# A transformer block's front, fed pair by pair: scale, shift and q weights in k-tile pairs, and no bias pass

## Chip, cores, metric

One core of a Trainium2 chip. The time is device microseconds (us) of one execution. Before the change: 841.25 us, median of three runs (841.21 to 841.26).

PE is the matmul engine, DVE the vector engine, ACT the scalar engine, POOL the GpSimd engine, SP the queue that issues DMA transfers. "Half clock" below means that the profile reads a granted PE clock of 0.50, or, where it reads 1.00 all the same, that matmuls start at half their pace. In the kernel before those of 512 columns start 0.426 us apart at a reading of 0.50 and 0.218 at 1.00. A *k-tile* is 128 of the 1024 rows over which a matmul sums, an *x tile* 128 rows of x. A *PSUM bank* is a buffer into which these kernels' matmuls add up; ACT and DVE read it out (an *evacuation*) before the program uses it again (in b1 PE waited 1.53 us for that). The *z matmuls* sum phi(k) over the rows; they are the first work after chunk 0's k and the first part of chunk 1's.

## The reference, cut to what matters

```python
x = A_x                                           # (1, 2048, 1024), bf16
mod = (silu(c) @ w_mod).reshape(1, 6, 1, -1)      # w_mod: (1024, 6144)
sa, ca, ga, sb, cb, gb = (mod[:, i] for i in range(6))
h = layernorm(x) * (1 + ca) + sa                  # ca: scale, sa: shift
qkv = h @ wqkv                                    # 32 heads of 32
# phi(q), phi(k), linear attention, @ wo, residual;
# then a second modulated layernorm and a SwiGLU block of width 3584
```

Only the first four lines' way into q matters here. The sequence is worked on in four chunks of 512 rows; the *front* is everything up to the end of chunk 0's q and k.

## The kernel before

Every instruction is recorded through a small helper that works out the waits, so all of them carry one line number (L178); the profile has to be read by tile names. The parts that the change touches:

```python
# loads, all on one queue, in this order
for st in range(4):
    P.dma("x0_%d" % st, XRES[:, st, :], xv[:, st, :])
P.dma("wca0", WCA[:, :, 0:512], wmv[:, :, D:D + 512])         # scale, rows of 1 KB
P.dma("wq0", WQK[:, 0:4, 0:512], wqkvv[:, 0:4, 0:512])
P.dma("wq1", WQK[:, 0:4, 512:D], wqkvv[:, 0:4, 512:D])
P.dma("wca1", WCA[:, :, 512:D], wmv[:, :, D + 512:2 * D])
P.dma("wq2", WQK[:, 4:8, 0:D], wqkvv[:, 4:8, 0:D])
P.dma("wsa", WSA[:], wmv[:, :, 0:D])                          # shift, rows of 2 KB
# ... x tiles 4, 5, first half of wk, x tiles 6, 7, second half of wk

def mod_sc(w, c0, ms):                 # silu(c) @ w_mod: matmuls of one column
    for m in ms:
        for kt in range(NDT):
            P.pe("matmul", out=PS[:, 0, c0 + m:c0 + m + 1], lhsT=w[:, kt, m * 128:(m + 1) * 128],
                 rhs=SILUC[:, kt:kt + 1], ...)

def q_bias(nts):                       # shift @ Wq, again one column each
    for nt in nts:
        for dt in range(NDT):
            P.pe("matmul", out=PS[:, 0, 16 + nt:17 + nt], lhsT=WQK[:, dt, nt * 128:(nt + 1) * 128],
                 rhs=MODTMP[:, dt:dt + 1], ...)
    P.dve("tensor_copy", out=BQ[...], in_=PS[...])

def q_phase_chunk0(side):              # q from h without the shift; the shift comes in as a bias
    lo, hi = [2, 0, 3, 1], [6, 4, 7, 5]
    for nt in range(7):
        q_part(nt, 1 + nt, lo)         # 4 matmuls 128x128x512 into PSUM bank 1 + nt
        if nt == 4:
            mod_sc(WCA, 8, range(4, NDT)); fin_ca(1)
            for dt in hi: h0_scale(dt, HT[:, 1, dt, :])
    for nt in range(6):
        q_part(nt, 1 + nt, hi)
    mod_sc(WSA, 0, range(NDT))
    act_stats(4); ...                  # LayerNorm statistics of x tiles 4, 5 (chunk 1)
    fin_sa()
    q_part(6, 7, hi)
    q_bias([0, 1])
    ...
    q_bias([2, 3, 4, 5, 6, 7])
    ...
    for dt in range(NDT):              # eight adds: k needs h with the shift
        P.dve("tensor_scalar", out=HT[:, 1, dt, :], in0=HT[:, 0, dt, :], scalar1=MODCOL[:, 1, dt:dt + 1], ...)
    for nt in range(2):
        phi_evac(1 + nt, PQT[:, nt, 0:512], bias=BQ[:, nt:nt + 1])   # ACT exp and relu, DVE min and add
    q_part(7, 1, range(NDT))           # needs bank 1 back
    for nt in range(2, 8): ...
```

Chunk 1 is prepared meanwhile: statistics, normalisation on DVE, a transposing DMA into tile `ht`, then eight scale/shift operations on `ht`, half on DVE and half on ACT.

## Time and profile before

| | before |
|---|---|
| time | 841.25 us |
| span of the profiled run | 839.5 us |
| first q matmul | 13.34 us |
| first k matmul of chunk 0 | 33.71 us |
| the first z matmul, after 80 k matmuls (64 of chunk 0, 16 of chunk 1) | 51.33 us |

The page of the kernel before: span, busy time of the engines, and the chain of work that ended last.

```profile
span 839.5 us, 10310 instructions
...
PE 827.5 (99%) x4211; PEld 384.3 (46%) x4291; DVE 295.9 (35%) x627; ACT 210.2 (25%) x363; POOL 41.3 (5%) x51
...
PE 94%; SPq 2%; DMA 1%; DVE 1%; issue 1%; ACT 0%; DVEq 0%; ACTq 0%
```

PE is busy 99% of the span and is 94% of the chain: the kernel is bound by matmuls nearly everywhere. A gain can only come from stretches where PE waits, does work that it need not do, or runs at half clock.

The stretches of the front. The columns are the stretch, its length, then busy us (and instructions) of PE, PE's weight loads, DVE, ACT and POOL, then the granted PE clock, the busy share of the DMA engines, and GB/s.

```profile
8.00:13.00 5.00, 3.79 (x67) 2.97 (x68) 3.47 (x15) 1.45 (x3) 2.04 (x3) 1.00 1.08 359
13.00:25.00 12.00, 11.92 (x84) 5.71 (x84) 2.37 (x9) 3.28 (x6) 0.00 (x0) 1.00 1.06 378
25.00:34.00 9.00, 8.13 (x143) 5.15 (x144) 5.88 (x24) 7.29 (x13) 0.74 (x1) 0.81 0.83 275
...
31.00:32.00 1.00, 1.00 (x3) 0.30 (x2) 1.00 (x5) 1.00 (x3) 0.42 (x1) 0.50 0.76 248
...
242.00:243.00 1.00, 1.00 (x6) 0.45 (x5) 0.62 (x3) 0.00 (x0) 1.00 (x3) 1.00 1.16 291
```

Two things to see. From 8 us on the DMA engines are full (a busy share of 1.06 to 1.08), at 359 to 378 GB/s. And around 31 us the granted clock is 0.50. The last line is from much later, where the only traffic is the gate and up weights, whose pieces have rows of 512 bytes: the engines are just as full (1.16) and move 291 GB/s. Single microseconds of this trace in which only 2 KB rows move (19 to 24 us) show 383 to 389, those with 1 KB rows (11 to 13 us) 348 and 349, about 350.

The timeline of PE for the front: start and length in us, then engine, operation, and tiles, and in brackets the idle time before, with what ended it. `siluc,wca` and `siluc,wsa` are the one-column matmuls for scale and shift, `modtmp,wqk` is the bias pass, `ht,wqk` is q, `wqk,ht` is k. The next start time minus this one, divided by the count, is the real pace; a group's length includes the tail of its last matmul (one of 512 columns is recorded as 0.379 us long on average).

```profile
13.34 4.52 PE L178 MATMUL ps<-ht,wqk 128*128 128x512 bf16 x20
...
25.41 1.74 PE L178 MATMUL ps<-siluc,wsa 128*128 128x1 bf16 x64
27.23 0.81 PE L178 MATMUL ps<-ht,wqk 128*128 128x512 bf16 x3
28.16 0.55 PE L178 MATMUL ps<-modtmp,wqk 128*128 128x1 bf16 x16
28.97 1.35 PE L178 MATMUL ps<-modtmp,wqk 128*128 128x1 bf16 x48 [0.26 <-DVE mv L178]
30.73 3.15 PE L178 MATMUL ps<-ht,wqk 128*128 128x512 bf16 x7 [0.41 <-ACT rl L178]
...
33.71 17.78 PE L178 MATMUL ps<-wqk,ht 128*128 128x512 bf16 x79
51.33 0.24 PE L178 MATMUL ps<-ones,pk_87 128*128 128x1 bf16 x4
```

Twenty q matmuls start over 4.36 us (13.34 to 17.70), 0.218 each; the k matmuls further on 0.216. The seven recorded in the line at 30.73 (eight are issued; some matmul records are missing from a trace) start over 2.98 us, 0.426 each: half clock. Before them lie 128 one-column matmuls and only four real ones.

The chain of waits of the kernel before also shows two pieces that are not PE:

```profile
46.15 0.80 ACT ht L178
...
47.81 1.52 ACT ht L178 x2
```

ACT is still scaling chunk 1's tile `ht` when PE gets there. The 80 k matmuls from 33.71 to 51.33 us take 17.62 us, 0.35 more than at 0.216 each.

### The profile page before, as it was taken

The numbers are of one execution on the slowest core, as the hardware profiler recorded it, in microseconds if no ns is written. First come the engines' busy times: TensorE is split into PE (matmuls) and PEld (weight loads), VectorE is DVE, ScalarE is ACT, GpSimd is POOL, SyncE is SP. The second block draws the span as 40 slices with busy tenths as digits, with TensorE's granted clock in tenths as the row PEclk, the third lists the DMA queues.
The fourth block names the chain that finished last, engine by engine and source line by source line (L and its number), as shares of the span: only waits on it lengthen the run. The fifth ranks groups of instructions, "written<-read, shape, count | busy, mean of one in ns | idle before, by whom it ended". The sixth has DMA issues, their size and how long they took to land.

```text
span 839.5 us, 10310 instructions
## 1 busy us (share of the span) xinstructions
PE 827.5 (99%) x4211; PEld 384.3 (46%) x4291; DVE 295.9 (35%) x627; ACT 210.2 (25%) x363; POOL 41.3 (5%) x51
## 2 busy tenths in 40 slices
PE   8999999999999999999999999999999999999998
PEld 4544444444444444444444444444444444444444
DVE  4677866656984211111221111022111202111111
ACT  5677763313333111100111111021111101111111
POOL 1000000000050000030000003000000300000000
PEclk9999999999999999999999999999999999999999
DMA  9792323746195895530355552045556204553000
GB/s 311 221 322 51 60 105 126 166 142 251 50 246 175 262 300 155 156 87 25 102 156 152 154 154 61 26 114 150 151 151 157 69 13 113 151 152 98 1 26 26
DMA packets 173391, 113.02 MB, mean 135 GB/s; under 512 B 32536, under 2 KB 156576, under 8 KB 173344
## 3 DMA queue, kind: packets, MB, share of 16 engines
q1 hardware_dynamic: 173344, 112.35, 47.4%
q8 instruction: 34, 0.56, 0.3%
q14 instruction: 13, 0.11, 0.0%
HBM read 100.67 MB, written 4.33 MB: 125 GB/s over the span
## 4 chain that ended last, share of the span: by engine, by line
PE 94%; SPq 2%; DMA 1%; DVE 1%; issue 1%; ACT 0%; DVEq 0%; ACTq 0%
PE ps L178 94%; SPq L178 2%; DMA xres<-in_A_x_dram 1%; DVE acc L178 0%; ACT ht L178 0%; DVE xres L178 0%; DVE mhl L178 0%; DVE stats L178 0%; ACT mw L178 0%; ACT e_92 L178 0%; DVE ve_72 L178 0%; ACT rl L178 0%; DVE ut L178 0%; DVE mv L178 0%; DVE mean_70 L178 0%
## 5 line engine op out<-in xcount | busy, mean ns | idle before, releaser
L178 DVE TENSOR_TENSOR at<-sg,ps 128x512 bf16<-128x512 bf16 x112 | 77.0, 687 | 296.2 <-PE ps L178 285.1
L178 ACT ACTIVATE sg<-ps 128x512 bf16<-128x512 f32 x112 | 66.9, 597 | 310.3 <-PE ps L178 298.9
L178 PE MATMUL ps<-wd_a,at 128*128 128x512 bf16 (+2 forms) x519 | 112.8, 372 | 0.5
L178 PE MATMUL ps<-wd_b,at 128*128 128x512 bf16 (+2 forms) x388 | 85.4, 372 | 0.5
L178 PEld LDWEIGHTS ps<-wd_a,at 128*128 128x128 bf16 x528 | 51.1, 98 | 59.8
L178 DVE TENSOR_TENSOR ut<-att,gb_b 128x512 bf16<-128x512 bf16 (+1 forms) x32 | 13.9, 434 | 167.3 <-ACT att L178 167.3
L178 ACT ACTIVATE att<-ps 128x512 bf16<-128x512 f32 (+1 forms) x32 | 17.4, 592 | 182.1 <-PE ps L178 182.1
L178 PEld LDWEIGHTS ps<-wd_b,at 128*128 128x128 bf16 x396 | 38.3, 98 | 44.6
L178 PE MATMUL ps<-ht,wqk 128*128 128x512 bf16 x248 | 57.8, 386 | 0.8 <-ACT rl L178 0.4
L178 PE MATMUL ps<-wqk,ht 128*128 128x512 bf16 x250 | 57.0, 379 | 0.5
L178 PE MATMUL ps<-mw,pqt 128*128 128x512 bf16 x250 | 55.8, 379 | 0.4
L178 PE MATMUL ps<-h2t,guu_117 128*128 128x512 bf16 x221 | 52.8, 379 | 0.2
L178 PE MATMUL ps<-h2t,guu_115 128*128 128x512 bf16 x219 | 52.6, 379 | 0.3
L178 PE MATMUL ps<-h2t,gug_114 128*128 128x512 bf16 x220 | 52.6, 379 | 0.2
L178 PE MATMUL ps<-h2t,guu_116 128*128 128x512 bf16 x221 | 52.6, 379 | 0.2
L178 PE MATMUL ps<-h2t,gug_111 128*128 128x512 bf16 x220 | 52.5, 379 | 0.2
L178 PE MATMUL ps<-h2t,gug_112 128*128 128x512 bf16 x219 | 52.5, 379 | 0.2
L178 PE MATMUL ps<-h2t,gug_113 128*128 128x512 bf16 x219 | 52.3, 379 | 0.3
L178 PE MATMUL ps<-h2t,guu_118 128*128 128x512 bf16 x217 | 52.1, 379 | 0.3
L178 POOL TENSOR_SCALAR h2t<-h2t,modcol 128x512 bf16<-128x512 bf16 x32 | 28.6, 911 | 395.8 <-DMA h2t<-xn_119 395.8
L178 ACT ACTIVATE e_92<-ps 128x512 bf16<-128x512 f32 x56 | 33.6, 600 | 27.0 <-PE ps L178 24.5
L178 PEld LDWEIGHTS ps<-mw,pqt 128*128 128x128 bf16 x256 | 24.9, 98 | 29.7 <-DVE xres L178 0.2
(123 smaller groups left out, 707.7 us busy)
## 6 DMA issues: line engine op xcount, KB each, us to landing
gug_111<-in_B_w_gate_dram SPq DMA_DIRECT2D x14, 512.0 KB, 4.0
guu_115<-in_B_w_up_dram SPq DMA_DIRECT2D x14, 512.0 KB, 5.3
gug_112<-in_B_w_gate_dram SPq DMA_DIRECT2D x14, 512.0 KB, 4.1
guu_116<-in_B_w_up_dram SPq DMA_DIRECT2D x14, 512.0 KB, 5.3
gug_113<-in_B_w_gate_dram SPq DMA_DIRECT2D x14, 512.0 KB, 4.0
guu_117<-in_B_w_up_dram SPq DMA_DIRECT2D x14, 512.0 KB, 5.3
gug_114<-in_B_w_gate_dram SPq DMA_DIRECT2D x14, 512.0 KB, 4.0
guu_118<-in_B_w_up_dram SPq DMA_DIRECT2D x14, 512.0 KB, 5.2
```

What stands on the lines that cost most here:

```text
L178: return getattr(e, method)(**kw)
```

## The change

The front is to be limited by PE alone: shift is added where scale is applied, so the bias pass goes (64 one-column matmuls and their waits), and so do the eight adds. For this, scale and shift must come early: they arrive in pairs of k-tiles with the q weights of that pair. q begins with two row tiles, at half width, as soon as pair 0 is there. Chunk 1's x is loaded before the k weights, and its scale/shift operations all go to DVE. The diff holds more than that: the last eight q matmuls use PSUM bank 0 instead of waiting for bank 1, the scaling of chunk 0 goes wholly to DVE, and statistics and later loads change places.

The core of the diff (cuts marked, lines shortened):

```diff
-        P.dma("wca0", WCA[:, :, 0:512], wmv[:, :, D:D + 512])
-        P.dma("wq0", ...)  P.dma("wq1", ...)  P.dma("wca1", ...)  P.dma("wq2", ...)
-        P.dma("wsa", WSA[:], wmv[:, :, 0:D])
+        def ca_load(p):
+            P.dma("wca%d" % p, WCA[:, :, 256 * p:256 * p + 256], wmv[:, :, D + 256 * p:D + 256 * p + 256])
+        def wq_load(p):
+            P.dma("wq%d" % p, WQK[:, 2 * p:2 * p + 2, 0:D], wqkvv[:, 2 * p:2 * p + 2, 0:D])
+        def sa_load(p):
+            P.dma("wsa%d" % p, WSA[:, :, 256 * p:256 * p + 256], wmv[:, :, 256 * p:256 * p + 256])
+        for p in range(4):
+            ca_load(p)
+            sa_load(p)
+            if p < 3:
+                wq_load(p)
+        # ... the last two q k-tiles one by one, x tiles 4 to 7, then wk
 ...
-        def q_bias(nts): ...
+        def mod_pair(p):
+            mod_sc(WCA, 8, range(2 * p, 2 * p + 2)); mod_sc(WSA, 0, range(2 * p, 2 * p + 2))
+            for f in fin_ca(p): f()                       # five small DVE operations
+            for dt in range(2 * p, 2 * p + 2): h0_scale(dt)   # scale and shift in one
 ...
         def q_phase_chunk0(side):
+            for nt in range(5):
+                q_part(nt, qb[nt], (0, 1), 0, 256)        # row tiles 0, 1 only
+            tile_transposes(2); tile_transposes(3)
+            ...
+            for nt in range(5):
+                if nt == 3: mod_pair(1)
+                q_part(nt, qb[nt], (0, 1), 256, 512)
+            for nt in range(5, 7): q_part(nt, qb[nt], (0, 1))
             for nt in range(7):
+                if nt == 4: mod_pair(2)
+                q_part(nt, qb[nt], (2, 3))
+            for nt in range(7):
+                if nt == 4: mod_pair(3)
+                q_part(nt, qb[nt], (4, 5))
+            act_stats(4); ...
+            for nt in range(6): q_part(nt, qb[nt], (6,))
+            for nt in range(7):
+                q_part(nt, qb[nt], (7,) if nt < 6 else (6, 7))
+                phi_evac(qb[nt], PQT[:, nt, 0:512])       # no bias
 ...
-            if dt % 2 == 0:
+            if dt % 2 == 0 or ch == 1:                    # chunk 1: all on DVE
 ...
-        warm(14)
+        warm(11, bank=3)                                  # warm-up matmuls, then wait for pair 0
```

More of the change, by code (lines that the diff above doesn't have):

```diff
@@ L396, in bass_adaLN_cond__linear_attn_block__swiglu_ffn__prompt_kernel @@
             P.dma("x0_%d" % st, XRES[:, st, :], xv[:, st, :])
-        P.dma("wca0", WCA[:, :, 0:512], wmv[:, :, D:D + 512])
-        P.dma("wq0", WQK[:, 0:4, 0:512], wqkvv[:, 0:4, 0:512])
-        P.dma("wq1", WQK[:, 0:4, 512:D], wqkvv[:, 0:4, 512:D])
-        P.dma("wca1", WCA[:, :, 512:D], wmv[:, :, D + 512:2 * D])
-        P.dma("wq2", WQK[:, 4:8, 0:D], wqkvv[:, 4:8, 0:D])
-        P.dma("wsa", WSA[:], wmv[:, :, 0:D])
-        for j in range(2):
+        def ca_load(p):
[9 more added lines that the diff above has]
+                wq_load(p)
+        for i in range(6, 8):
+            P.dma("wq%d" % i, WQK[:, i, 0:D], wqkvv[:, i, 0:D])
+        for j in range(4):
             P.dma("x1_%d" % j, XRES[:, 4 + j, :], xv[:, 4 + j, :])
-        P.dma("wk0", WQK[:, :, 1024:1536], wqkvv[:, :, 1024:1536])
-        for j in range(2, 4):
-            P.dma("x1_%d" % j, XRES[:, 4 + j, :], xv[:, 4 + j, :])
+        for i in range(2):
+            P.dma("wk0%d" % i, WQK[:, 4 * i:4 * i + 4, 1024:1536], wqkvv[:, 4 * i:4 * i + 4, 1024:1536])
         P.dma("wk1", WQK[:, :, 1536:2048], wqkvv[:, :, 1536:2048])
@@ L437, in bass_adaLN_cond__linear_attn_block__swiglu_ffn__prompt_kernel @@
         P.act("activation", out=SILUC[:], in_=PSB[:, 1, 0:NDT], func=ACT.Silu)
-        P.act("activation", out=ACTWARM[:], in_=SILUC[:], func=ACT.Exp)
         P.dve("tensor_copy", out=SILUF[:], in_=SILUC[:])
@@ L468, in th_dma @@
         def th_dma(st):
-            buf, j = (st // 4 + 1) % 2, st % 4
+            buf, j = (st // 4) % 2, st % 4
             xbar(HT[:, buf, :, j * 128:(j + 1) * 128], XRES[:, st, :])
         def th_mod(ch, dt):
-            buf = (ch + 1) % 2
-            if dt % 2 == 0:
+            buf = ch % 2
+            if dt % 2 == 0 or ch == 1:
                 P.dve("tensor_scalar", out=HT[:, buf, dt, :], in0=HT[:, buf, dt, :], scalar1=MODCOL[:, 0, dt:dt + 1],
@@ L488, in mod_sc @@
                     mod_first[0] = False
-        def fin_ca(h):
-            sl, sp = slice(4 * h, 4 * h + 4), slice(8 + 4 * h, 12 + 4 * h)
-            P.dve("tensor_copy", out=MODTMP[:, sp], in_=PS[:, 0, sp])
-            P.dve("tensor_scalar", out=MODTMP[:, sp], in0=MODTMP[:, sp], scalar1=1.0, scalar2=None, op0=ALU.add)
-            P.dve("tensor_copy", out=MODCOL[:, 0, sl], in_=MODTMP[:, sp])
-        def fin_sa():
-            P.dve("tensor_copy", out=MODTMP[:, 0:8], in_=PS[:, 0, 0:8])
-            P.dve("tensor_copy", out=MODCOL[:, 1, :], in_=MODTMP[:, 0:8])
@@ L500, in q_bias, with fin_ca @@
-        def q_bias(nts):
-            for nt in nts:
-                for dt in range(NDT):
-                    P.pe("matmul", out=PS[:, 0, 16 + nt:17 + nt], lhsT=WQK[:, dt, nt * 128:(nt + 1) * 128],
-                         rhs=MODTMP[:, dt:dt + 1], start=False, stop=(dt == NDT - 1), skip_group_check=True)
-            P.dve("tensor_copy", out=BQ[:, nts[0]:nts[-1] + 1], in_=PS[:, 0, 16 + nts[0]:17 + nts[-1]])
-        def h0_scale(dt, src):
-            if dt % 4 < 2:
-                P.act("activation", out=HT[:, 0, dt, :], in_=src, func=ACT.Copy, scale=MODCOL[:, 0, dt:dt + 1])
-            else:
-                P.dve("tensor_scalar", out=HT[:, 0, dt, :], in0=src, scalar1=MODCOL[:, 0, dt:dt + 1],
-                      scalar2=None, op0=ALU.mult)
+        def fin_ca(p):
+            sl, sp = slice(2 * p, 2 * p + 2), slice(8 + 2 * p, 10 + 2 * p)
+            return [
+                lambda: P.dve("tensor_copy", out=MODTMP[:, sp], in_=PS[:, 0, sp]),
+                lambda: P.dve("tensor_copy", out=MODTMP[:, sl], in_=PS[:, 0, sl]),
+                lambda: P.dve("tensor_scalar", out=MODTMP[:, sp], in0=MODTMP[:, sp], scalar1=1.0, scalar2=None,
+                              op0=ALU.add),
+                lambda: P.dve("tensor_copy", out=MODCOL[:, 1, sl], in_=MODTMP[:, sl]),
+                lambda: P.dve("tensor_copy", out=MODCOL[:, 0, sl], in_=MODTMP[:, sp]),
+            ]
@@ new lines, in mv_pair, with t_view, h0_first @@
+        def mv_pair(p):
+            mod_sc(WCA, 8, range(2 * p, 2 * p + 2))
+            mod_sc(WSA, 0, range(2 * p, 2 * p + 2))
+        def mod_pair(p):
+            mv_pair(p)
+            for f in fin_ca(p):
+                f()
+            for dt in range(2 * p, 2 * p + 2):
+                h0_scale(dt)
+        def t_view(dt, n=1):
+            return PSB[:, 6 + dt // 4, (dt % 4) * 256:(dt % 4 + n) * 256]
+        def h0_first(dt, half, eng):
+            dst = HT[:, 0, dt, 256 * half:256 * half + 256]
+            if eng == "act":
+                P.act("activation", out=dst, in_=t_view(dt), func=ACT.Identity, scale=MODCOL[:, 0, dt:dt + 1],
+                      bias=MODCOL[:, 1, dt:dt + 1])
+            else:
+                P.dve("tensor_scalar", out=dst, in0=t_view(dt), scalar1=MODCOL[:, 0, dt:dt + 1],
+                      scalar2=MODCOL[:, 1, dt:dt + 1], op0=ALU.mult, op1=ALU.add)
@@ new lines, in raw_copy, with h0_scale @@
+        def raw_copy(dt, n, half, eng):
+            dst = HT[:, 1, dt:dt + n, 256 * half:256 * half + 256]
+            src = t_view(dt, n).rearrange("p (d q) -> p d q", q=256)
+            if eng == "act":
+                P.act("activation", out=dst, in_=src, func=ACT.Copy)
+            else:
+                P.dve("tensor_copy", out=dst, in_=src)
+        def h0_scale(dt):
+            P.dve("tensor_scalar", out=HT[:, 0, dt, :], in0=HT[:, 1, dt, :], scalar1=MODCOL[:, 0, dt:dt + 1],
+                  scalar2=MODCOL[:, 1, dt:dt + 1], op0=ALU.mult, op1=ALU.add)
@@ L528, in bass_adaLN_cond__linear_attn_block__swiglu_ffn__prompt_kernel, with act_stats @@
         junk0 = HT[:, 1, 0:2, :]
-        def act_stats(st):
-            for fn_, acc_ in ((ACT.Identity, SUMX), (ACT.Square, SUMSQ)):
-                P.act("activation", out=junk0, in_=XRES[:, st, :].rearrange("p (a b) -> p a b", a=2), func=fn_,
-                      accum_out=acc_[:, st:st + 1])
+        def act_stats(st, c0=0):
+            n = (D - c0) // 512
+            for fn_, sc_, acc_ in ((ACT.Identity, 1.0 / D, SUMX), (ACT.Square, D ** -0.5, SUMSQ)):
+                P.act("activation", out=junk0[:, 0:n, :], in_=XRES[:, st, c0:D].rearrange("p (a b) -> p a b", a=n),
+                      func=fn_, scale=sc_, accum_out=acc_[:, st:st + 1])
@@ L535, in act_mv_ops @@
         def act_mv_ops(st):
             return [
-                lambda: P.dve("tensor_scalar", out=MV[:, st, 0:1], in0=SUMX[:, st:st + 1], scalar1=1.0 / D, scalar2=None,
-                              op0=ALU.mult),
-                lambda: P.dve("tensor_tensor", out=MSQ2[:, st:st + 1], in0=MV[:, st, 0:1], in1=MV[:, st, 0:1], op=ALU.mult),
-                lambda: P.dve("scalar_tensor_tensor", out=MV[:, st, 1:2], in0=SUMSQ[:, st:st + 1], scalar=1.0 / D,
-                              in1=MSQ2[:, st:st + 1], op0=ALU.mult, op1=ALU.subtract),
-            ]
@@ L544, in bass_adaLN_cond__linear_attn_block__swiglu_ffn__prompt_kernel, with neg_rstd @@
-        act_stats(0)
-        act_stats(3)
-        s1_, s2_ = ln1_stats_ops(1), ln1_stats_ops(2)
-        m0, m3 = act_mv_ops(0), act_mv_ops(3)
+                lambda: P.dve("tensor_copy", out=MV[:, st, 0:1], in_=SUMX[:, st:st + 1]),
+                lambda: P.dve("scalar_tensor_tensor", out=MV[:, st, 1:2], in0=SUMX[:, st:st + 1],
+                              scalar=SUMX[:, st:st + 1], in1=SUMSQ[:, st:st + 1], op0=ALU.mult, op1=ALU.subtract),
+            ]
+        def neg_rstd(st):
+            P.dve("tensor_scalar", out=VE[:, st:st + 1], in0=MV[:, st, 1:2], scalar1=-1.0, scalar2=EPS, op0=ALU.mult,
+                  op1=ALU.add)
+            P.pool("tensor_tensor", out=RSTD[:, st:st + 1], in0=VE[:, st:st + 1], in1=NEGHALF[:, 0:1], op=ALU.pow)
@@ new lines, in mixed_mv_ops @@
+        def mixed_mv_ops(st):
+            return [
+                lambda: P.dve("bn_aggr", out=MV[:, st, :], in_=STATS[:, (st // 4) % 2, st % 4, 0:1, :]),
+                lambda: P.dve("scalar_tensor_tensor", out=MSQ2[:, st:st + 1], in0=MV[:, st, 0:1], scalar=MV[:, st, 0:1],
+                              in1=MV[:, st, 1:2], op0=ALU.mult, op1=ALU.add),
+                lambda: P.dve("scalar_tensor_tensor", out=MV[:, st, 0:1], in0=MV[:, st, 0:1], scalar=0.5,
+                              in1=SUMX[:, st:st + 1], op0=ALU.mult, op1=ALU.add),
+                lambda: P.dve("scalar_tensor_tensor", out=SUMSQ[:, st:st + 1], in0=MSQ2[:, st:st + 1], scalar=0.5,
+                              in1=SUMSQ[:, st:st + 1], op0=ALU.mult, op1=ALU.add),
+                lambda: P.dve("scalar_tensor_tensor", out=MV[:, st, 1:2], in0=MV[:, st, 0:1], scalar=MV[:, st, 0:1],
+                              in1=SUMSQ[:, st:st + 1], op0=ALU.mult, op1=ALU.subtract),
+            ]
@@ new lines, in bass_adaLN_cond__linear_attn_block__swiglu_ffn__prompt_kernel, with tile_transposes @@
+        act_stats(2)
+        act_stats(3, 512)
+        s0_, s1_, s3_ = ln1_stats_ops(0), ln1_stats_ops(1), ln1_stats_ops(3)
+        m2, m3 = act_mv_ops(2), mixed_mv_ops(3)
+        def tile_transposes(j):
+            for dt in range(NDT):
+                c = (dt % 4) * 256 + (j % 2) * 128
+                P.pe("transpose", out=PSB[:, 6 + dt // 4, c:c + 128], in_=XRES[:, j, dt * 128:(dt + 1) * 128],
+                     identity=IDENT[:])
+        warm(11, bank=3)
+        mod_sc(WCA, 8, range(2))
@@ L548, in bass_adaLN_cond__linear_attn_block__swiglu_ffn__prompt_kernel @@
+        warm(3, bank=3)
+        fa = fin_ca(0)
+        s0_[0]()
+        s0_[1]()
         s1_[0]()
+        s0_[2]()
+        ln1_rstd1(0)
         s1_[1]()
-        s2_[0]()
+        ln1_xn(0)
+        tile_transposes(0)
         s1_[2]()
-        m0[0]()
         ln1_rstd1(1)
-        m0[1]()
-        s2_[1]()
-        m0[2]()
-        ln1_rstd1(0)
-        s2_[2]()
+        s3_[0]()
+        m2[1]()
+        m2[0]()
+        m3[0]()
+        neg_rstd(2)
+        fa[0]()
         ln1_xn(1)
-        ln1_rstd1(2)
@@ L561, in bass_adaLN_cond__linear_attn_block__swiglu_ffn__prompt_kernel @@
-        ln1_xn(0)
-        m3[0]()
+        fa[2]()
         m3[1]()
+        fa[4]()
+        m3[2]()
+        mod_sc(WSA, 0, range(2))
+        tile_transposes(1)
+        m3[3]()
+        m3[4]()
+        fa[1]()
+        neg_rstd(3)
+        fa[3]()
+        h0_first(0, 0, "dve")
+        h0_first(1, 0, "dve")
+        raw_copy(4, 4, 0, "act")
+        raw_copy(2, 2, 0, "dve")
         ln1_xn(2)
-        m3[2]()
-        ln1_rstd1(3)
         ln1_xn(3)
-        def th_transposes_j(j):
-            for dt in range(NDT):
-                P.pe("transpose", out=PSB[:, 4 + dt // 2, (dt % 2) * 512 + j * 128:(dt % 2) * 512 + (j + 1) * 128],
-                     in_=XRES[:, j, dt * 128:(dt + 1) * 128], identity=IDENT[:])
@@ L574, in bass_adaLN_cond__linear_attn_block__swiglu_ffn__prompt_kernel @@
-        warm(14)
-        for n, j in enumerate((1, 0, 2)):
-            th_transposes_j(j)
-            warm(0)
-        mod_sc(WCA, 8, range(4))
-        th_transposes_j(3)
-        warm(4)
-        fin_ca(0)
-        for dt in range(4):
-            h0_scale(dt, PSB[:, 4 + dt // 2, (dt % 2) * 512:(dt % 2) * 512 + 512])
-        for dt in range(4, NDT):
-            src = PSB[:, 4 + dt // 2, (dt % 2) * 512:(dt % 2) * 512 + 512]
-            if dt % 4 < 2:
-                P.act("activation", out=HT[:, 1, dt, :], in_=src, func=ACT.Copy)
-            else:
-                P.dve("tensor_copy", out=HT[:, 1, dt, :], in_=src)
@@ L610, in phi_flush, with q_part @@
             phi_pend.clear()
-        def q_part(nt, bank, dts):
-            dts = list(dts)
+        def q_part(nt, bank, dts, c0=0, c1=512):
             for dt in dts:
-                P.pe("matmul", out=PS[:, bank, :], lhsT=WQK[:, dt, nt * 128:(nt + 1) * 128],
-                     rhs=HT[:, 0, dt, :], start=(dt in (0, 2) and dt == dts[0]), stop=(dt == dts[-1] and dt in (5, 7)))
+                P.pe("matmul", out=PS[:, bank, c0:c1], lhsT=WQK[:, dt, nt * 128:(nt + 1) * 128],
+                     rhs=HT[:, 0, dt, c0:c1], start=(dt == 0 and c0 == 0), stop=(dt == 7), skip_group_check=True)
         qk_ctr = [0]
@@ L625, in q_group @@
         def q_group(ch, nt):
-            buf, bank = (ch + 1) % 2, next_bank()
+            buf, bank = ch % 2, next_bank()
             for dt in range(NDT):
@@ L633, in k_group @@
             st = 4 * ch + j
-            buf, bank = (ch + 1) % 2, next_bank()
+            buf, bank = ch % 2, next_bank()
             lo = D + h * 512
@@ L684, in q_phase_chunk0 @@
         def q_phase_chunk0(side):
-            lo, hi = [2, 0, 3, 1], [6, 4, 7, 5]
+            qb = [1, 2, 3, 4, 5, 6, 7]
+            for nt in range(5):
+                q_part(nt, qb[nt], (0, 1), 0, 256)
+            tile_transposes(2)
+            tile_transposes(3)
+            for dt in range(2):
+                h0_first(dt, 1, "dve")
+            raw_copy(4, 4, 1, "act")
+            raw_copy(2, 2, 1, "dve")
+            P.act("activation", out=ACTWARM[:], in_=SILUC[:], func=ACT.Exp)
+            for nt in range(5):
+                if nt == 3:
+                    mod_pair(1)
+                q_part(nt, qb[nt], (0, 1), 256, 512)
+            for nt in range(5, 7):
+                q_part(nt, qb[nt], (0, 1))
             for nt in range(7):
-                q_part(nt, 1 + nt, lo)
                 if nt == 4:
-                    mod_sc(WCA, 8, range(4, NDT))
-                    fin_ca(1)
-                    for dt in hi:
-                        h0_scale(dt, HT[:, 1, dt, :])
-            for nt in range(6):
-                q_part(nt, 1 + nt, hi)
-            mod_sc(WSA, 0, range(NDT))
+                    mod_pair(2)
+                q_part(nt, qb[nt], (2, 3))
+            for nt in range(7):
+                if nt == 4:
+                    mod_pair(3)
+                q_part(nt, qb[nt], (4, 5))
             act_stats(4)
@@ L698, in q_phase_chunk0 @@
                 f()
-            fin_sa()
-            for nt in range(6, 7):
-                q_part(nt, 1 + nt, hi)
-            q_bias([0, 1])
+            ln1_rstd1(5)
             for f in act_mv_ops(4):
                 f()
-            q_bias([2, 3, 4, 5, 6, 7])
-            ln1_rstd2(4)
-            for dt in range(NDT):
-                P.dve("tensor_scalar", out=HT[:, 1, dt, :], in0=HT[:, 0, dt, :], scalar1=MODCOL[:, 1, dt:dt + 1],
-                      scalar2=None, op0=ALU.add)
-            for nt in range(2):
-                phi_evac(1 + nt, PQT[:, nt, 0:512], bias=BQ[:, nt:nt + 1])
-            q_part(7, 1, range(NDT))
-            for nt in range(2, 8):
-                phi_evac([1 + nt, 1][nt == 7], PQT[:, nt, 0:512], bias=BQ[:, nt:nt + 1])
+            neg_rstd(4)
+            ln_ops[2][0]()
+            for jj in range(2):
+                ln1_xn(4 + jj)
+                th_dma(4 + jj)
+            for nt in range(6):
+                q_part(nt, qb[nt], (6,))
+            for nt in range(7):
+                q_part(nt, qb[nt], (7,) if nt < 6 else (6, 7))
+                phi_evac(qb[nt], PQT[:, nt, 0:512])
                 for f in side.get(nt, []):
                     f()
-            qk_ctr[0] = 1
+            q_part(7, 0, range(NDT))
+            phi_evac(0, PQT[:, 7, 0:512])
+            for f in side.get(7, []):
+                f()
+            qk_ctr[0] = 0
         def add(d, k, f):
@@ L728, in ln_x1 @@
             ln1_rstd1(4 + jj)
-        for jj in range(2):
-            add(qside, 2, lambda jj=jj: ln1_xn(4 + jj))
-            add(qside, 2, lambda jj=jj: th_dma(4 + jj))
-        for f_ in ln_ops[2]:
-            add(qside, 2, f_)
-        for f_ in ln_ops[3]:
-            add(qside, 3, f_)
+        add(qside, 1, ln_ops[2][1])
+        add(qside, 1, ln_ops[2][2])
+        add(qside, 3, ln_ops[3][0])
+        add(qside, 3, ln_ops[3][1])
+        add(qside, 3, ln_ops[3][2])
         add(qside, 3, lambda: ln1_rstd2(6))
@@ L739, in bass_adaLN_cond__linear_attn_block__swiglu_ffn__prompt_kernel @@
             add(qside, 5, lambda jj=jj: th_dma(4 + jj))
-        add(qside, 6, late_loads)
+        add(kside, 1, late_loads)
         for dt in range(NDT):
-            add(kside, 3 + dt // 4, lambda dt=dt: th_mod(1, dt))
+            add(kside, 3 + dt // 2, lambda dt=dt: th_mod(1, dt))
         q_phase_chunk0(qside)
```

## The prediction

> **What bounds it now.** The page gives a span of 839.5 us with PE busy 99%; the chain of waits is 94% PE. Only the front is touched. In the timeline the first q matmul starts at 13.3 us, the k matmuls of chunk 0 at 33.7 us. These 20.4 us hold 64 q matmuls (64 x 0.216 = 13.8 us), three blocks of one-column matmuls (scale's 2nd half 0.95, shift 1.75, bias 1.9 us), about 1.2 us of waits, and a half-speed clock: the one-microsecond windows show PEclk 0.64, 0.50, 0.50, 0.65 from 30 to 34 us, and eight matmuls there take 0.427 us each (1.7 us lost). [...] here a window of nearly only one-column matmuls was followed by 3.4 us at half clock[...].
>
> The DMA engines are full too: 350 to 390 GB/s from 8 to 31 us. The 7 MB needed for q (x0, scale, shift, q weights) have landed at 25.2 us.
>
> **What the change does.**
> - Removes: the bias pass (1.9 us of PE, and waits), eight DVE adds (2.2 us), very probably the half-clock stretch (1.7 us), and the bias operand of 16 q evacuations (ACT pitch 0.57 to 0.49 us).
> - Adds: shift is needed pair by pair; a half-width start; 16 transposes inside the q phase (about 1 us).
> - Moves: scale and shift come in rows of 512 B instead of 1 and 2 KB. The windows show 350 GB/s with 1 KB rows, 387 with 2 KB rows, and 291 where the gate and up weights (512 B rows) load alone (241 to 250 us). [...] So these 4 MB take about 14.4 us instead of 11.4, q weights 5.4 instead of 5.7: the last q weights land 2.7 us later, near 27.9 us.
>
> **Critical path (estimate from these durations).** With landing about 2 us behind the mean bytes moved, as before: scale/shift pair 0 near 11.5, pair 1 near 16.5, pair 2 near 21.4, pair 3 near 26.4 us. PE has about 4 us of work per pair and DMA needs 5, so PE becomes DMA-bound, idling 1 us per pair. First q matmul near 13.2 us (no earlier). After the last shift piece: 0.5 us of one-column matmuls, then 28 matmuls, 6.05 us: k starts near 33.0 us, against 33.7. The PE work removed (3.6 us) is thus mostly handed to waiting for DMA. ACT and DVE have less work, so chunk 1 should follow without its present small wait (0.2 to 0.4 us). The remaining 790 us do not change.
>
> Predicted gain 0.9 us: 840.3 us; range 838.0 to 842.5. Faster by over 2%: 0.01; within 2%: 0.98; slower: 0.01.
>
> **What would show it.** Windows 8 to 27 us near 300 to 330 GB/s; PE idle before the one-column matmuls, released by DMA; no PEclk below 1 from 30 to 34 us; first k matmul at 32 to 34 us; no wait of PE for ht near 47 to 49 us; from 60 us on the same stretches, shifted equally.
>
> **What would make it wrong.** 512 B rows running near 350 GB/s in the mix: then PE stays the bound, k starts near 31 us, the gain is about 3 us. Waits for DMA long enough to halve the clock in mid q (near 10 us a half-clock window is likely and harmless): up to 2 us worse. The LayerNorm statistics of tile 4, ahead of the q evacuations on ACT, delaying PSUM banks; or chunk 1's eight scale/shift operations, all on DVE, arriving after 47 us: 1 to 2 us worse.

841.25 less the gain of 0.9 us is 840.3, as predicted. The trace before shows one half-clock stretch, after 128 one-column matmuls and four of 512 columns; that it comes from them, and that another might come near 10 us or after waits for DMA, was the estimate. Half clock near a wait for DMA was measured only later: at 8.9 to 15.7 us in the changed kernel, whose PE waited 2.75 us until 9.38, and at 21.8 to 25.2 us in the third trace, after a wait of 1.29 us.

## The result

840.68 us median (840.48 to 841.45, four runs) against 841.25 (841.21 to 842.43, four runs). The ratio is 0.9992, 95% interval 0.9974 to 1.0009: the same within 2%, and not clear of zero. (A ratio is the mean time of one kernel's runs over that of the other's in the same rounds, so not quite the ratio of the medians.) The changed kernel was timed twice more beside the experiments, five rounds' worth each: 840.19 against 841.88 (ratio 0.9983, 0.9969 to 0.9996) and 840.38 against 842.05 (0.9981, 0.9969 to 0.9994). So by the medians it is faster by 0.6 to 1.7 us, less than a quarter of a per cent, and clear of zero in the two later jobs.

The same views of the changed kernel. The page:

```profile
span 838.5 us, 10210 instructions
...
PE 825.3 (98%) x4154; PEld 384.1 (46%) x4233; DVE 298.3 (36%) x641; ACT 203.8 (24%) x355; POOL 41.0 (5%) x52
...
PE 95%; SPq 2%; DMA 1%; DVE 1%; issue 1%; ACT 0%; DVEq 0%
```

The stretches of the front:

```profile
8.00:13.00 5.00, 3.62 (x50) 2.80 (x51) 2.51 (x16) 2.12 (x6) 1.15 (x3) 0.59 1.14 321
13.00:25.00 12.00, 11.32 (x125) 7.06 (x126) 5.64 (x22) 3.54 (x4) 0.41 (x1) 0.89 1.14 316
25.00:34.00 9.00, 8.77 (x69) 4.30 (x69) 5.88 (x21) 5.49 (x11) 1.06 (x2) 1.00 1.05 352
...
31.00:32.00 1.00, 1.00 (x6) 0.41 (x5) 0.82 (x3) 1.00 (x3) 1.00 (x2) 1.00 1.07 355
```

The DMA engines are busier than before (1.14 against 1.06 to 1.08) and move less: 321 and 316 GB/s where it was 359 and 378. The half clock at 31 us is gone. But a new one has come: 0.59 in the first stretch and 0.89 in the second. By half-microsecond windows it lasts from 8.9 to 15.7 us.

The timeline of PE:

```profile
2.76 3.87 PE L178 MATMUL ps<-e_92,ident 128*128 128x512 bf16 x11 [0.37 <-DVE e_92 L178]
9.38 0.59 PE L178 MATMUL ps<-siluc,wca 128*128 128x1 bf16 x16 [2.75 <-DMA wca<-in_w_mod_dram]
...
13.59 2.29 PE L178 MATMUL ps<-ht,wqk 128*128 128x256 bf16 x10 [0.19 <-DVE ht L178]
...
17.06 1.04 PE L178 MATMUL ps<-ht,wqk 128*128 128x256 bf16 x6 [0.28 <-DVE ht L178]
...
25.80 0.54 PE L178 MATMUL ps<-siluc,wca 128*128 128x1 bf16 x16
26.52 0.55 PE L178 MATMUL ps<-siluc,wsa 128*128 128x1 bf16 x16 [0.18 <-DMA wsa<-in_w_mod_dram]
26.93 6.31 PE L178 MATMUL ps<-ht,wqk 128*128 128x512 bf16 x27
33.08 17.43 PE L178 MATMUL ps<-wqk,ht 128*128 128x512 bf16 x79
50.35 0.24 PE L178 MATMUL ps<-ones,pk_87 128*128 128x1 bf16 x4
```

PE stops at 6.6 us and waits 2.75 us for the first scale piece. The first q matmul comes at 13.59, no earlier than before. The ten half-width matmuls start over 2.13 us (what follows them starts at 15.72), where the ten of a2, at a granted clock of 1.00, take 1.22 (13.06 to 14.28). The last shift piece lands at 26.5 us and is waited for, but only for 0.18 us. k starts at 33.08 instead of 33.71, 0.63 us earlier, and the first z matmul comes at 50.35 instead of 51.33, 0.98 earlier. That is the whole difference of the spans (839.5 and 838.5): later stretches are shifted by 1.0 us and otherwise equal.

The chain of waits of the changed kernel, from the issue of the last shift piece:

```profile
17.89 8.58 DMA wsa<-in_w_mod_dram
...
26.52 2.84 PE ps L178 x26
```

The ACT pieces at 46 to 49 us have left the chain, and the landing of the last shift piece, 8.58 us after its issue began, has come in. The 80 k matmuls now take 17.27 us, 0.216 each.

### The profile page after: what moved, and what is told of

Its sections match the earlier page's. It is cut to its first block, busy times and chain, and to the rows that moved or that the text cites. A ratio compares the mean times of both kernels' runs of the same rounds, so it can differ in the third digit from the quotient of the medians.

```text
span 838.5 us, 10210 instructions
## 1 busy us (share of the span) xinstructions
PE 825.3 (98%) x4154; PEld 384.1 (46%) x4233; DVE 298.3 (36%) x641; ACT 203.8 (24%) x355; POOL 41.0 (5%) x52
## 4 chain that ended last, share of the span: by engine, by line
PE 95%; SPq 2%; DMA 1%; DVE 1%; issue 1%; ACT 0%; DVEq 0%
PE ps L178 95%; SPq L178 2%; DMA wsa<-in_w_mod_dram 1%; DVE acc L178 0%; DVE xres L178 0%; DVE mhl L178 0%; ACT mw L178 0%; DVE ve_72 L178 0%; DVE ut L178 0%; DVE mean_70 L178 0%; DVE msq_71 L178 0%; DVE sumx L178 0%; DVEq L249 0%
## 5 line engine op out<-in xcount | busy, mean ns | idle before, releaser
L178 PE MATMUL ps<-ht,wqk 128*128 128x512 bf16 (+1 forms) x258 | 58.4, 376 | 1.0 <-DVE ht L178 0.5
L178 ACT ACTIVATE e_92<-ps 128x512 bf16<-128x512 f32 x64 | 39.1, 611 | 30.8 <-PE ps L178 27.0
L178 ACT ACTIVATE rl<-ps 128x512 bf16<-128x512 f32 x64 | 38.9, 608 | 0.0
```

Of the source, the lines that this page charges most:

```text
L178: return getattr(e, method)(**kw)
```

## The experiments

Eleven runs were made, nine of edited kernels and two of the changed kernel as it is. The theory was the prediction's: rows of 512 bytes make PE wait for DMA, and this eats what the removed work gives. The rivals: the half clock at the start; the bytes or their order, not the row length; a second limit in chunk 1.

| run | what | first k matmul, us | median, us | ratio to before (95%) |
|---|---|---|---|---|
| (after) | the changed kernel | 33.08 | 840.68 | 0.9992 (0.9974 to 1.0009) |
| a1_rows2k | after, same bytes in 2 KB rows (wrong) | 32.05 | 839.02 | 0.9962 (0.9944 to 0.9980) |
| a2_warm | after, 11 more warm-up matmuls | 33.42 | 840.65 | 0.9988 (0.9973 to 1.0003) |
| a3_rows2k_warm | both (wrong) | 31.10 | 838.70 | 0.9964 (0.9947 to 0.9980) |
| b1_nobias | before without bias pass (wrong) | 32.61 | 840.05 | 0.9978 (0.9963 to 0.9993) |
| after_again | after | 32.47 | 840.19 | 0.9983 (0.9969 to 0.9996) |
| b2_rows512 | before, scale and shift in 512 B rows | 36.50 | 845.27 | 1.0039 (1.0027 to 1.0052) |
| b3_spread | before, q matmuls spread | 35.12 | 843.07 | 1.0014 (1.0001 to 1.0026) |
| m2_mix_warm | after, pairs 2 and 3 joined, warm | 37.03 | 844.05 | 1.0025 (1.0013 to 1.0038) |
| after_third | after | 33.11 | 840.38 | 0.9981 (0.9969 to 0.9994) |
| b4_fill | before, five useless matmuls in the waits | 32.45 | 841.24 | 0.9997 (0.9984 to 1.0011) |
| b5_fill_early | the same, chunk 1 earlier | 32.84 | 842.25 | 1.0003 (0.9990 to 1.0015) |

The first k matmul is read from the one profiled execution; the median is over all runs of the job. The kernel before spread from 840.7 to 842.7 us in these jobs, so differences of the medians below about 0.5 us carry nothing.

The three kernels that are wrong passed the comparison with the reference all the same: the scale and shift are so small here (w_mod's entries are drawn near 0.05/32) that a mistake in them stays within its tolerance. That is no proof that this part is right.

### Row length and the half clock at the start: a1, a2, a3

a1_rows2k keeps everything but the shape of the pieces:

```diff
-WCA[:, :, 256 * p:256 * p + 256], wmv[:, :, D + 256 * p:D + 256 * p + 256]
+WCA[:, 2 * p:2 * p + 2, :], wmv[:, 2 * p:2 * p + 2, D:2 * D]      # the shift likewise
-lhsT=w[:, kt, m * 128:(m + 1) * 128]
+lhsT=w[:, m, kt * 128:(kt + 1) * 128]                             # a block of its own piece: wrong result
```

> The changed kernel with one difference: each scale and shift piece is taken as two k-tile rows of 2 KB instead of 256 columns of 512 B (same bytes, same order, same waits, same instruction count; result wrong on purpose, as the one-column matmuls then read the wrong blocks). Theory (row length makes PE wait for DMA): the pieces land earlier, last shift piece near 22.5 to 23.5 us instead of 26.5; PE becomes the bound; because the half-clock stretch of 9 to 15.6 us stays, first k matmul near 31.8 us instead of 33.1, time about 839.4 us (1.0 to 1.5 below the changed kernel). Rival (the half-clock stretch at the start, not DMA, sets when q ends): k starts at 33.0 again, time unchanged at 840.6. Rival (bytes, not row length): landing times unchanged.

The stretch in which the after kernel moved 316 GB/s, for a1_rows2k:

```profile
13.00:25.00 12.00, 11.68 (x126) 7.31 (x126) 4.92 (x21) 3.23 (x4) 0.00 (x0) 1.00 1.05 387
```

387 GB/s for the same bytes in the same order. The last shift piece, issued at 10.6 us, landed at most 12.4 us later, at 23.0, instead of 26.5. In its waits of PE, the only line for scale or shift weights is the first piece:

```profile
PE ps L178 <- DMA wca<-in_w_mod_dram: 1.0, 1, 1.0
```

k starts at 32.05, near the 31.8 expected, and the median is 2.8 us below that of the kernel before in the same rounds, where the changed kernel is 0.6 to 1.7 below it. (One of its four runs took 836.52; why is not known, as only one run has a trace. The other three are 838.5 to 839.6.) The rival "bytes, not row length" is refuted for the landing times. What the rows cost in time this run alone does not show well: in the changed kernel's own traces the first scale piece comes at 8.4 to 9.4 us (here 8.63) and k at 32.47 to 33.11, so a1's k is only 0.4 us below the earliest of them. a3 against a2 below is the clean comparison. a1's half-width matmuls still start 0.21 us apart, where a2's start 0.12 us apart, so PE is at half clock at the start here too, although the clock column of this trace shows 1.00.

a2_warm changes one number, `warm(11, bank=3)` to `warm(22, bank=3)`.

> The changed kernel with 11 more warm-up matmuls in the gap of 6.6 to 9.4 us, so that the clock should not halve there. Theory: PEclk is 1 from 6.5 us on, q gets ahead, then waits longer for DMA; the last shift piece still lands at 26.5 us and k still starts at 33.0 (within 0.2), time within 0.3 us of the changed kernel. Rival (the half-clock stretch costs the gain): k starts near 31.5, time 1.5 us lower.

Three lines of its PE timeline:

```profile
22.25 0.55 PE L178 MATMUL ps<-siluc,wsa 128*128 128x1 bf16 x16 [1.13 <-DMA wsa<-in_w_mod_dram]
...
26.85 0.55 PE L178 MATMUL ps<-siluc,wsa 128*128 128x1 bf16 x16 [0.55 <-DMA wsa<-in_w_mod_dram]
...
34.86 16.58 PE L178 MATMUL ps<-wqk,ht 128*128 128x512 bf16 x76 [0.42 <-DMA wqk<-in_A_wqkv_dram]
```

The ten half-width matmuls now start 0.12 us apart, at a granted clock of 1.00, and q gets 1.4 us ahead (second half at 15.62 instead of 17.06), and then PE gives all of it back: 1.13 us of waiting for a shift piece, 0.55 for the next, 0.42 for k weights. k starts at 33.42, the time is 840.65. So taking away the half clock at the start alone gains nothing here: behind it stands DMA.

a3_rows2k_warm is both edits.

> Both of the above together (result wrong on purpose). Theory: neither DMA nor clock holds PE now, k starts near 30.2 us, time about 837.7 to 838.3 us if chunk 1 keeps up. If only one of the two mattered, this equals the better of the two alone.

k starts at 31.10, earlier than either alone, though 0.9 us later than expected: the first q matmul came at 12.97 where I had reckoned with about 12.3, and my sum for the rest was too small as well. The median, 838.7, is 0.3 below a1's, within the spread; the trace separates the two better than the times do. Against a2, where the clock is up as well, the row length makes 2.3 us at the first k matmul (31.10 against 33.42), 2.9 us in the span (836.6 against 839.5) and 1.95 us in the medians. Neither alone is the limit of the changed kernel. Both reach the end of q within about a microsecond of each other: 32.05 us with the half clock alone (a1), 33.42 with the 512-byte rows alone (a2).

### The kernel before with single parts of the change: b1, b2

b1_nobias drops the two `q_bias` calls and sets the bias to zero.

> The kernel before without the bias pass (64 one-column matmuls and their waits; bias zero, result wrong on purpose), loads as they were. Theory: this is the gain that the change aimed at: PE loses 1.9 us of matmuls, some 1 us of waits and, if the clock no longer halves at 30 us, 1.7 us: first k matmul near 29.5 to 30.5 us instead of 33.7. But the total should drop by less, since chunk 1's transposed tile is ready only at 49.4 us there and PE would then wait for it from about 44 us: time 840.5 to 841.2. Rival (nothing else binds): time near 837.5.

The expectation of k at 29.5 to 30.5 us failed: 32.61. Two things came in the place of the bias pass. The last eight q matmuls need bank 1, and ACT empties it only after the statistics of x tile 4: PE waited 1.53 us for it.

```profile
29.41 3.36 PE L178 MATMUL ps<-ht,wqk 128*128 128x512 bf16 x8 [1.53 <-ACT rl L178]
```

And the clock halved all the same, from 29.0 to 32.4 us. The wait for chunk 1 that I expected did not come either, since k started late and ACT was done with chunk 1's tile at 47.3 us, where it had been 49.3. Still, the total falls by 1.8 us (ratio 0.9978): dropping the bias pass alone, with a wrong result, is worth as much as the whole rebuild.

b2_rows512 is the other side: the loads of the kernel before, cut into 256-column pieces in the old order, and nothing else.

> The kernel before with one part of the change alone: scale and shift fetched in 256-column pieces (512 B rows), same order, same bytes, nothing else. Theory (512 B rows cost about 3 us over these 4 MB): the last shift piece lands near 28 us instead of 25.2, k starts near 36.2 us instead of 33.7, time 2 to 2.5 us above the kernel before. Rival (row length costs nothing that matters): within 0.3 us of the kernel before.

One line of its DVE timeline, then three of PE:

```profile
29.30 1.29 DVE L178 BATCH_NORM_STATS2 stats<-xres 128x6 f32<-128x512 bf16 x2 [9.27 <-DMA xres<-in_A_x_dram]
...
30.92 0.58 PE L178 MATMUL ps<-modtmp,wqk 128*128 128x1 bf16 x16 [1.46 <-DVE modtmp L178]
...
33.12 3.60 PE L178 MATMUL ps<-ht,wqk 128*128 128x512 bf16 x8
36.50 18.07 PE L178 MATMUL ps<-wqk,ht 128*128 128x512 bf16 x80
```

k starts at 36.50, 0.3 later than expected, and the time rises by 3.4 us (845.27 against 841.88). The eight matmuls before k are at half clock again, and this time it lasts 6.8 us (31.0 to 37.8), 1.3 us of it under k, about 0.65 us lost by an estimate from these two times. The way was not the expected one, though. No wait of PE for a shift piece is recorded here. What waited was DVE: in program order the statistics of x tile 5 stand ahead of the shift's cast, x tile 5 comes behind the shift on the queue, and it landed at 29.3 us instead of 26.5. So the bias pass began 2.76 us later (30.92 instead of 28.16), and that is nearly all of the 2.79 us by which k is late. The chain of waits of the kernel before goes the same way, through x tile 5. The 512-byte rows alone cost the kernel before 3.4 us, twice what the rebuild as a whole gains, but that is the price on this path.

### The half clock: b3, m2, b4

b3_spread moves two groups of four q matmuls:

```diff
-            for nt in range(6):
+            for nt in range(5):
                 q_part(nt, 1 + nt, hi)
             mod_sc(WSA, 0, range(NDT))
 ...
-            for nt in range(6, 7):
-                q_part(nt, 1 + nt, hi)
+            q_part(5, 6, hi)
             q_bias([0, 1])
+            q_part(6, 7, hi)
```

> The kernel before with two groups of q matmuls held back and put between the one-column matmuls (4 real ones before the first bias part, 4 before the second); same work. Theory: the waits there (about 1 us) are filled and the clock no longer halves from 30 to 34 us (the eight matmuls before k take 0.216 us each); k starts near 32.5 us instead of 33.7, time 0.5 to 1.2 us below the kernel before, so the same as the whole rebuild reached. If the clock halves all the same, the gain is at most 0.3 us.

It made things worse: k at 35.12, 843.07 us. The shift weights land at 25.7 us; with fewer matmuls in front of them PE waits 0.93 us for them, then does 64 one-column matmuls, and the clock halves at 27.9, earlier than in the kernel before, and stays so for 6.8 us. With real work moved away from in front of the shift's 64 one-column matmuls, the stretch there without real matmuls became longer by the 0.93 us of waiting.

m2_mix_warm was meant as a better version: pieces of 256, 256 and 512 columns, so that half of the scale and shift comes in 1 KB rows, with the warm-up of a2.

> A try at a better correct version: the changed kernel with the last two pairs of scale and shift joined into one piece of 512 columns each (1 KB rows, fetched before the last q weights), and 11 more warm-up matmuls. Theory: half of the 4 MB moves at 350 instead of 291 GB/s and the last shift piece lands near 22.6 us; PE is then the bound after it; k starts near 32.5 us, time 0.3 to 0.6 us below the changed kernel. If row length didn't matter, no gain beyond noise.

Three lines of its PE timeline:

```profile
24.29 1.01 PE L178 MATMUL ps<-siluc,wsa 128*128 128x1 bf16 x32 [2.05 <-DMA wsa<-in_w_mod_dram]
25.17 12.03 PE L178 MATMUL ps<-ht,wqk 128*128 128x512 bf16 x42
37.03 17.43 PE L178 MATMUL ps<-wqk,ht 128*128 128x512 bf16 x80
```

The last shift piece landed at 24.3 us, not 22.6 (earlier than the changed kernel's 26.5 all the same), and PE stood idle for 2.05 us before it, after 32 one-column matmuls and another wait of 0.56. The clock halved at 24.05 and came back at 30.9: the 42 q matmuls start over 11.86 us instead of 9.1. k at 37.03, 844.05 us. With the 2.05 us of waiting for DMA came a half clock that cost 2.8 us more.

b4_fill is the opposite of b3 in the kernel before: it puts useless matmuls where PE waits.

```diff
+        P.dve("memset", ap=E1[:, 3, :], constant=0.0)
 ...
             q_part(6, 7, hi)
+            fill(3)                  # matmuls that add zeros to bank 7
             q_bias([0, 1])
+            fill(2)
```

> The kernel before with five useless matmuls (zeros added to a bank) in the two waits around the first bias part: three ahead of it, two after it. Nothing else. Theory A ([...] the half-clock stretch costs 1.7 us or more): the eight matmuls ahead of k take 0.216 us, k starts near 32.2 us instead of 33.7. But chunk 1's transposed tile is not ready before 49 us in this kernel, and k of chunk 0 now ends at 46, so PE waits 2 to 3 us for ht and the total drops by 0.5 us at most. Theory B (chunk 1 is not a second limit): the total drops by 1.5 us. Theory C (the clock halves for another reason): k starts at 33.9 or later, total unchanged or worse.

(The reason that theory A gave is cut, as no run shows it; theory C's "another reason" is one other than that. Theory A's forecast is kept: with matmuls in the two waits the clock does not halve.)

Four lines of its PE timeline:

```profile
30.94 1.67 PE L178 MATMUL ps<-ht,wqk 128*128 128x512 bf16 x7 [0.21 <-issue]
32.45 7.07 PE L178 MATMUL ps<-wqk,ht 128*128 128x512 bf16 x32
39.82 8.43 PE L178 MATMUL ps<-wqk,ht 128*128 128x512 bf16 x36 [0.30 <-ACT rl L178]
49.31 2.82 PE L178 MATMUL ps<-wqk,ht 128*128 128x512 bf16 x11 [1.06 <-ACT ht L178]
```

Theory A's forecast holds in the main. From 13 us on the clock never halves in this trace (it reads 1.00 in every half microsecond to 40 us), k starts at 32.45, 1.26 us earlier than before with *more* work on PE. And then PE waits 1.06 us for ACT to finish chunk 1's `ht` (the trace shows the same wait in smaller pieces on the weight loads from 46.9 us on), and 0.30 for a PSUM bank. The 80 k matmuls take 19.51 us (32.45 to 51.96), 2.2 more than at 0.216 each. The total is 841.24 against 842.05 in the medians, but one of the five runs took 843.49; the ratio is 0.9997 (0.9984 to 1.0011): no gain that can be told from noise. That the clock stayed up is no accident of one trace: all five runs of b4 and all five of b5, which has the same fill, have a mean granted clock of 1.000, while all 25 runs of the kernel before in these jobs have 0.996 or 0.998. (Such a mean can miss a stretch, as in a1, so the pace in b4's trace is the stronger evidence.)

b5_fill_early tried to lift that second limit too: statistics, normalisation and transposes of x tiles 6 and 7 two evacuations earlier, chunk 1's scale/shift on DVE as in the changed kernel.

> The run above, and chunk 1 made ready earlier: the statistics of x tiles 6 and 7 and their normalisation and transposes are put two q evacuations earlier in program order, and the eight scale/shift operations of chunk 1 are all on DVE, two per k group, as in the changed kernel. Theory A: k at 32.2 us, ht ready near 47 us, the wait for ht mostly gone; 1.3 to 2.0 us below the kernel before, equal to or just below the changed kernel with none of its rebuild. Theory B: no gain over the run above.

One line of its PE timeline:

```profile
41.87 10.52 PE L178 MATMUL ps<-wqk,ht 128*128 128x512 bf16 x47 [1.96 <-ACT rl L178]
```

The wait for `ht` is gone and a wait of 1.96 us for a bank has taken its place: DVE's earlier work delayed the q evacuations (ACT stood idle for 2.47 us ahead of 39.30, waiting for DVE), so ACT gave bank 1 back late. 842.25 us. Theory B's "no gain" is what was measured, but not for B's reason: chunk 1 *is* a second limit, and the evacuations are a third right behind it.

### The changed kernel again: after_again, after_third

> The changed kernel again, unedited, in the rounds of the runs beside it, as the mark to compare them with and to see the spread. Expected: 840.3 to 841.0 us, 0.5 to 1.2 below the kernel before; k starts at 33.0 to 33.4 us.

> The changed kernel unedited, as the mark beside the next two. Expected: 0.6 to 1.7 us below the kernel before, as in its two earlier jobs; k starts between 32.4 and 33.4 us.

The times came out as expected or, for after_again, 0.1 us lower (840.19, and 1.7 below the kernel before where 0.5 to 1.2 was expected); k started at 32.47, earlier than expected, and at 33.11. The third trace took another way to the same end. Lines of its PE timeline:

```profile
8.41 0.55 PE L178 MATMUL ps<-siluc,wca 128*128 128x1 bf16 x16 [0.78 <-DMA wca<-in_w_mod_dram]
...
11.80 1.38 PE L178 MATMUL ps<-ht,wqk 128*128 128x256 bf16 x10 [0.60 <-DVE ht L178]
...
21.04 0.55 PE L178 MATMUL ps<-siluc,wsa 128*128 128x1 bf16 x16 [1.29 <-DMA wsa<-in_w_mod_dram]
```

The first scale piece landed 1 us earlier, the clock did not halve at the start, q began at 11.80. Then PE waited 1.29 us for a shift piece and the clock halved in mid q, from 21.8 to 25.2. k started at 33.11 all the same. So one program has at least two patterns of half clock from run to run. What q's end hangs on differs as well. The last DMA piece in the chain of waits of after_again, then of after_third:

```profile
3.07 5.80 DMA wca<-in_w_mod_dram
...
11.98 9.01 DMA wsa<-in_w_mod_dram
```

In after_again that is the first scale piece: from 8.9 us on PE, with small steps of DVE, ran at its own pace, at half clock at first (its half-width matmuls start 0.21 us apart), and waited for no shift piece. In after_third it is the third shift piece, at 21.0, and what follows is PE at half clock. Only in the first trace is it the last shift piece, at 26.5.

## Why the prediction was right

Predicted 840.3 us in a range of 838.0 to 842.5; measured 840.68, and 840.19 and 840.38 later.

- **Row length.** Right for the transfers. 300 to 330 GB/s were predicted for 8 to 27 us; 321 and 316 were measured. The last shift piece was put at 26.4 us; it landed at 26.5. a1, with the same bytes in 2 KB rows and 387 GB/s, shows that the row length causes it. Its price is 2.3 us at the first k matmul where the clock is up (a2 against a3) and 3.4 us in the kernel before (b2, by way of x tile 5); I had the weights land 2.7 us later. But only one of three traces of the changed kernel has the last shift piece as the limit.
- **Start of q.** Predicted 13.2 us; 13.59, 13.13 and 11.80 in three traces. "No earlier" was too strong, but the early start in the third trace changed nothing.
- **Start of k.** Predicted 33.0; 33.08, 32.47 and 33.11.
- **Chunk 1's wait for ht** gone: right, 0.35 us, from 17.62 to 17.27 us for the 80 matmuls.
- **The rest unchanged**: right, the spans differ by the 0.98 us seen at the first z matmul.
- **"PE becomes DMA-bound, idling 1 us per pair."** This step failed as written. In the first two traces PE waited for the later pairs 0.18 us or not at all, because it had already spent the slack at half clock in the first pair. I had called a half-clock window near 10 us likely and harmless; it lasted 6.8 us, to 15.7. Harmless it was, in that removing it gained nothing (a2), but it, and not idling, is what filled the time. The wait of about 1 us for a piece shows in a2 and in the third trace. The sum came out right because PE at half clock and DMA with 512-byte rows reach the end of q within about a microsecond of each other. The prediction did not foresee that; that the number came out so close is luck in this part.
- **The half clock of the kernel before.** That it follows from one-column matmuls and short waits was the estimate from one trace, and no run shows a cause by itself. What b4 shows is that with five useless matmuls in the waits the clock reads 1.00 throughout, and k starts 1.26 us earlier. Not foreseen was that removing the bias pass would not be enough to prevent it (b1).

So where did the expected gain go? The change removed 1.9 us of bias pass and the half clock that followed, about 3.6 us. It took back 2 to 3 us by fetching scale and shift in 512-byte rows (a2 against a3: 1.95 us in the medians, 2.9 in the spans). Of the three limits in the kernel before (bias and clock, chunk 1's tile, the banks) it moved all three: its traces show no wait of PE for a bank or for chunk 1's `ht` before 50 us. This is probably why it keeps its gain of about 1 us where b4, which moves one, shows none; no run takes the three apart in the changed kernel.

What stays open: why the time of one kernel varies by up to 2 us between runs. The runs differ in the mean granted clock (0.998 or 0.996, by the records that a run keeps; 0.002 of 839 us is one stretch of 3.4 us at half clock), but in the kernel before the runs with 0.996 are not reliably the slower ones, and a1's trace shows that such records can be missing.

No version was found that beats the changed kernel with a right result. a1 and a3, whose medians are 1.2 to 2.0 us below the changed kernel's, show what more there would be if the pairs could come in 2 KB rows, but a pair of k-tiles of scale *is* 256 columns of w_mod, 512 bytes of each row.

## What to carry to other kernels

When a load is cut finer so that work can start earlier, price the new row length from a stretch of the same trace where such rows move alone (here 291 GB/s with 512 B rows, about 350 with 1 KB, 383 to 389 with 2 KB), before counting the gain. Before removing work from a bound engine, find what stands right behind it: here each single limit that was lifted (b4, b5, a2) handed its time to the next one. And look at PE's waits: in m2 a wait of 2.05 us after 32 one-column matmuls came with a half clock that cost 2.8 us more, and in b4 five useless matmuls in the waits brought k forward by 1.26 us, though not the total.

## What the traces show of rows and clock

- Full DMA engines moved 291 GB/s with 512 B rows (kernel before, 242 to 243 us), 348 and 349 with 1 KB (11 to 13 us) and 383 to 389 with 2 KB (19 to 24 us); all are loads from HBM to SBUF on one core, from the SP queue. Going from 1 and 2 KB rows to 512 B cost the kernel before 3.4 us (b2).
- The half-clock stretches that the clock column shows lasted 3.4 us (before, b1, third trace) or 6.8 us (after, b2, b3, m2). From the start of the shift's one-column matmuls to the q matmuls ahead of k, the kernel before had 128 one-column matmuls, short waits and four matmuls of 512 columns (25.41 to 30.73 us), and the clock halved at 30.2; b4 had nine such matmuls there (25.44 to 30.94 us), and it did not halve. No run shows what makes the difference beyond these five matmuls.
- The clock column does not show every such stretch. It reads 1.00 for a1, where half-width matmuls start 0.21 us apart (0.12 in a2), and in the traces of both kernels at the start, where warm-up matmuls of 512 columns start 0.43 us apart (from 2.75 to 5.7 us in the kernel before, to 5.3 in the changed one) and q matmuls later 0.218. The distance of the starts is the better evidence.
